# Merging a block-diagonal matrix into a weight: full float32r products by masked blocks, or float32 blocks of 32x32 side by side

## The chip, the cores and the metric

The kernel runs on one core of one Trainium2 chip. Its time is device microseconds for one execution; the time before is the median of three runs. TensorE is called PE (its weight loads PEld), VectorE DVE, ScalarE ACT, GpSimd POOL, and SyncE's queue SP.

## The reference

A layer norm of x, a linear attention with 32 heads of 32 channels, and a gated SwiGLU branch of the same normed x; their product is added to x:

```python
def reference(A_x, A_wqkv, A_wo, B_x, B_w1, B_w3, B_w2):
    def _A_ref(x, wqkv, wo):                      # x: 1 x 2048 x 1024
        H = 32; Dh = D // H
        q, k, v = ...                             # x @ wqkv, by heads
        phi = lambda t: jnp.where(t > 0, t + 1, jnp.exp(t)) + 1e-6
        pq, pk = phi(q), phi(k)
        kv = jnp.einsum("bhsd,bhse->bhde", pk, v)
        z = jnp.einsum("bhsd->bhd", pk)
        num = jnp.einsum("bhqd,bhde->bhqe", pq, kv)
        den = jnp.einsum("bhqd,bhd->bhq", pq, z)[..., None] + 1e-6
        o = num / den
        return o.transpose(0, 2, 1, 3).reshape(B, S, D) @ wo
    def _B_ref(x, w1, w3, w2):                    # w1, w3: 1024 x 3584
        ...
        return (silu(gate) * up) @ w2
    xn = _layernorm(x)
    s = _A_ref(xn, A_wqkv, A_wo)
    g = _silu(_B_ref(xn, B_w1, B_w3, B_w2))
    return x + s * g                              # x is A_x, before the norm
```

`kv` is one 32x32 matrix for each head. Because `o @ wo` is `(pq * 1/den) @ (blockdiag(kv) @ wo)`, the kernel first multiplies kv into wo (1024 x 1024), head by head, and calls that the merge.

## The kernel before, in words

Matmuls of the large products work on pairs of float32r numbers. `split` rounds a tile to a high part on ACT and takes the rest on DVE, and `mm3` issues three 128x128 by 128x512 matmuls: high by high, high by low, low by high (lines 109, 110, 111). The large products are done by a two-by-two scheme of seven products instead of eight; `PRODUCTS` = B11, T2, T3, T1, B21, T4, B22 names the right operands. They are B11, B21, B22 themselves and T1 = B12 - B11, T2 = B22 - T1, T3 = B22 - B12, T4 = B21 - T2.

The work goes through two halves of the rows of x. In the second half, queries and keys are followed by `row_products`, which makes the sums behind kv (kept in DRAM as `g_d`), and then by 14 pairs of `gemm`s for the gate and the up branch, each 7 x 12 = 84 full matmuls. A gemm takes banks of PSUM for its five accumulators, one (`ba`) at its start and four (`bb` to `be`) after its first product; operands of the next gemms are staged through further banks by `advance`. PSUM has eight banks in one pool (`ps`), shared by all.

Beside the gemms run jobs. They are generators; after each but the last of a gemm's seven products, `catch_up` lets the first job of the list go on to its next `yield`. One such step is called a turn here; a gemm has six. `attention_work` is the job that follows the row products. It divides the queries of the first row groups by their denominators (`divide`), makes and merges kv, and goes on with the other divisions; weight sums follow. `go_on` runs a list of `Job`s and asks for the loads of the next ones two or three ahead. Loads go to `job_tile`s, of which there are four, through SP's queue.

The merge before takes the eight column groups j one after another. `key_values(j)` multiplies g by the value weights as float32 matmuls of 128 x 32 weights, four of them side by side (line 1323, `tile_position=(0, g * DH)`), and DVE spreads the four 32x32 results under a mask `hmask` into a 128x128 block-diagonal `kvf`. `merge_wo` splits `kvf` and a 128-row strip of wo (`wos`), does one `mm3` for each half of the columns, and copies the result back to SBUF (`wo`, line 1356). When both strips of a k are there, POOL makes the four T's (`sums_of`, lines 1145 to 1149) and SP stores the seven products to `wp_d`, one DRAM tile for each four of them. When the second half is over, `attention_right` loads them (line 1623), and they are split into the right operands of the attention's last product.

The denominators (line 1258) are another group of small float32 matmuls: weights of 128 x 32, 256 columns, four side by side. The order of instructions on an engine is fixed when the kernel is built, by a planner that takes the code's order as priority.

Of the kernel before, what the change touches and what calls it, by code (L numbers as in the profile page):

```python
# [22 lines left out]
def tile_linear_attention_times_swiglu(  # L23
# [31 lines left out]
    make_identity(nc, ident)  # L55
    eps = const.tile([P, 1], F32, name="tiny")
    nc.vector.memset(eps, 1e-6)
    hmask = const.tile([P, P], F32, name="hmask")
    nc.vector.memset(hmask, 0.0)
    for i in range(P // DH):  # L60
        nc.vector.memset(hmask[i * DH:(i + 1) * DH, i * DH:(i + 1) * DH], 1.0)
# [19 lines left out]
    WROWS = [9, 6, 13, 24, 15, 11, 10, 21, 1, 16, 4, 18, 5, 8, 12, 20, 17, 25]  # L81
    WBLOCKS = {0: (1, 1), 2: (1, 0), 3: (2, 1), 7: (2, 0), 14: (0, 1), 22: (3, 0), 19: (2, 0), 23: (2, 1)}
    h_d = [dram.tile([P, len(HROWS), 2, NQ, P], F32, name=f"h_d{h}") for h in range(NH)]
    wp_d = [dram.tile([P, 4, C], F32, name=f"wp_d{g}") for g in range(7 * ND // 8)]
    wt_d = [dram.tile([P, len(WROWS), C], F32, name=f"wt_d{k}") for k in range(NQ)]
    qs_d = [dram.tile([P, 7, ND // 2, P], F32, name=f"qs_d{m}") for m in range(S // (2 * P))]
    r_d = [dram.tile([P, 2 * P], F32, name=f"r_d{m}") for m in range(S // (2 * P))]
# [517 lines left out]
                if next(job, None) is None:  # L605
                    jobs.pop(0)

    held = [0]

    def advance():  # L610
        if held[0]:
# [4 lines left out]
    def gemm(B, A, use, early=False, paired=False, own=False, led=False):  # L616

        name = B.name
        stays = name[0] == "u"

        B.upto("B11")
        u = (st.tile([P, C], F32, tag="own", bufs=1, name=f"u{name}") if own else
             pe.tile([P, C], F32, tag="u", name=f"u{name}"))
        ba = bank(f"a{name}")  # L630
        last = product(ba, B.upto("B11"), A["A11"], True)
        if early:
            yield
        copied = nc.scalar.copy(out=u, in_=ba)
        if early:
            yield
            product(ba, B.upto("B21"), A["A12"], False)
            yield
            yield from use.steps(0, 0, ba)
            yield  # L640
        else:
            advance()
            catch_up(copied, last)
            if paired:
                yield
        bb, bc, bd, be = (bank(f"{n}{name}") for n in "bcde")

        def settled(*marks):
            if not led:
                advance()  # L650
                catch_up(*marks)

        last = product(bb, B.upto("T2"), A["S2"], True)
        if led:
            yield
        added = nc.vector.tensor_add(out=u, in0=bb, in1=u)
        settled(copied, added, last)
        if paired or led:
            yield
        last = product(bc, B.upto("T3"), A["S3"], True)  # L660
        if led:
            yield
        c21 = small(f"c21{name}")
        c22 = bc if stays else small(f"c22{name}")
        added = nc.vector.tensor_add(out=c21, in0=bc, in1=u)
        settled(copied, added, last)
        if paired or led:
            yield
        last = product(bd, B.upto("T1"), A["S1"], True)
        if led:  # L670
            yield
        added = nc.vector.tensor_add(out=c22, in0=bd, in1=c21)
        if led:
            yield
        use(1, 1, c22)
        advance()
        catch_up(copied, added, last)
        if paired:
            yield
        if not early:  # L680
            last = product(ba, B.upto("B21"), A["A12"], False)
            use(0, 0, ba)
# [457 lines left out]
        store_rows(h, t, 16, r16)  # L1140
        yield

    def sums_of(b11, b12, b21, b22, e=nc.gpsimd):

        e.tensor_sub(out=b11, in0=b12, in1=b11)
        e.tensor_sub(out=b12, in0=b22, in1=b12)
        yield True
        e.tensor_sub(out=b22, in0=b22, in1=b11)
        e.tensor_sub(out=b21, in0=b21, in1=b22)

    def weight_sums(t, part, place=job_tile, e=pool, queue=nc.sync, slow=False):

        cols = slice(part * P, (part + 1) * P)
# [145 lines left out]

        return Job(load, steps)  # L1300

    kvf = {}

    def key_values(j):

        def load():
            g = job_tile([P, 2, ND // 2, P], f"g{j}")
            for e in range(2):
                nc.sync.dma_start(out=g[:, e], in_=g_d[2 * e + j % 2][:, :, j // 2 * P:(j // 2 + 1) * P])
            w = job_tile([P, 2, ND // 2, P], f"wv{j}")  # L1310
            rows = wqkv[:, 2 * D + j * P:2 * D + (j + 1) * P]
            nc.sync.dma_start(out=w.rearrange("p e k n -> p (e k) n"), in_=rows.rearrange("(k p) n -> p k n", p=P))
            return g, w

        def steps(both):
            yield True
            acc = bank(f"kv{j}")[:, :DH]
            g_, w_ = both
            for e in range(2):
                for k in range(ND // 2):  # L1320
                    for g in range(P // DH):
                        c = slice(g * DH, (g + 1) * DH)
                        nc.tensor.matmul(acc[c], lhsT=w_[:, e, k, c], rhs=g_[:, e, k, c], skip_group_check=True,
                                         start=e + k == 0, stop=bool(e) and k == ND // 2 - 1, tile_position=(0, g * DH))
# [6 lines left out]
        return [Job(load, steps)]  # L1331

    def merge_wo(k):

        both = []

        def load(e):
            j = k + e * (ND // 2)
            t = job_tile([P, 2, C], f"wo{j}")
            nc.sync.dma_start(out=t, in_=wo[j * P:(j + 1) * P, :].rearrange("p (n c) -> p n c", c=C))  # L1340
            return t

        def steps(e, t):
            both.append(t)
            j = k + e * (ND // 2)
            kvm = st.tile([P, 2, P], FR, tag="kvm", bufs=1, name=f"kvm{j}")
            split(kvm, kvf[j])
            o = []
            for n in range(2):
                o.append(operand([P, 2, C], FR, f"wos{j}_{n}"))  # L1350
                split(o[n], t[:, n])
                yield True
            for n in range(2):
                acc = bank(f"wp{j}_{n}")
                mm3(acc, (kvm[:, 0], kvm[:, 1]), (o[n][:, 0], o[n][:, 1]), True, True)
                nc.scalar.copy(out=t[:, n], in_=acc)
                yield True
            if e:
                b = [t[:, n] for t in both for n in range(2)]
                for n, i in (("B11", 0), ("B21", 2), ("B22", 3)):  # L1360
                    store(n, b[i])
                yield from sums_of(*b)
                for n, i in (("T1", 0), ("T3", 1), ("T4", 2), ("T2", 3)):
                    store(n, b[i])
                yield True

        def store(n, t):
            g, e = divmod(7 * k + PRODUCTS.index(n), 4)
            nc.sync.dma_start(out=wp_d[g][:, e], in_=t)

        return [Job(lambda e=e: load(e), lambda t, e=e: steps(e, t)) for e in range(2)]


    def all_denominators():
        yield from spread_z()
# [242 lines left out]
    def attention_right(n, i, k):  # L1618
        g, e = divmod(k * len(PRODUCTS) + i, 4)
        if g not in places:  # L1620
            raw = praw.tile([P, 4, C], F32, tag="raw", name=f"wpr{g}")
            for i in range(2):
                nc.sync.dma_start(out=raw[:, 2 * i:2 * i + 2], in_=wp_d[g][:, 2 * i:2 * i + 2])
            places[g] = raw, pa.tile([P, 4, 2, C], FR, tag=AOPS[g], name=f"wp{g}")
        return places[g][0][:, e]

# [186 lines left out]
```

## Time and profile before

| what | value |
|---|---|
| time, median of 3 runs (lowest to highest) | 2263.08 us (2261.74 to 2263.15) |
| the profiled execution | 2261.58 us, span 2259.8 us |
| busy: PE, PEld, DVE, ACT, POOL | 99%, 82%, 69%, 46%, 31% of the span |
| merge and key-values run | 1110 to 1300 us |
| merged weight stored, loaded | 1123.1 to 1300.3 us, 1581.0 to 1614.3 us |
| DMA | 495.18 MB, mean 219 GB/s |

Times in rows of the profile are microseconds from the span's start unless marked ns. A row of a group of instructions gives line, engine, operation, output and inputs, the count behind x, and the durations. A row of the timeline gives start, duration and what ran; in brackets stands the idle time before it and what ended that. SPq and ACTq rows are DMAs being issued, not their transfer. A matmul's duration includes the depth of its pipeline, so matmuls overlap in the record.

### The profile page before, as it was taken

What the parts mean: (1) busy time and instruction counts of PE and PEld (TensorE: products, weight loads), DVE (VectorE), ACT (ScalarE), POOL (GpSimd) and SP (SyncE); (2) the same over time, 40 slices, a digit from 0 to 9 for tenths busy, and PEclk for the clock granted to TensorE, in tenths of its full rate; (3) what the DMA queues carried; (4) which work ended last, traced back from release to release, by engine and by line L of the source; (5) the groups of instructions that cost most, each with busy time, mean ns of one, the idle gap of its engine ahead of it and who ended that gap; (6) DMA issues with size and microseconds to landing.
All of it is one profiled execution on the core that took longest, in us unless ns stands there. A gap on an engine that the chain in (4) does not pass through costs nothing.

```text
span 2259.8 us, 31282 instructions
## 1 busy us (share of the span) xinstructions
PE 2240.6 (99%) x10584; PEld 1844.9 (82%) x10584; DVE 1553.4 (69%) x2607; ACT 1044.8 (46%) x1780; POOL 696.5 (31%) x1163
## 2 busy tenths in 40 slices
PE   7999999999999999999999999999999999999998
PEld 6888888888888888778888888888888888888887
DVE  8987777665656776567766687856865555566576
ACT  6655454534343555434445443443522544444452
POOL 2220223377773621001244255478121000001010
PEclk9999999999999999999999999999999999999999
DMA  6555655677778745777766577877776856668595
GB/s 242 175 198 173 192 176 180 186 226 211 215 217 273 243 143 194 255 253 240 226 200 195 178 237 246 246 220 226 252 225 212 303 196 220 221 204 268 194 302 204
DMA packets 434657, 495.18 MB, mean 219 GB/s; under 512 B 22192, under 2 KB 328112, under 8 KB 434384
## 3 DMA queue, kind: packets, MB, share of 16 engines
q1 hardware_dynamic: 352112, 353.44, 49.4%
q0 software_dynamic: 26080, 82.99, 11.2%
q10 hardware_dynamic: 56304, 56.76, 8.0%
q8 instruction: 83, 1.36, 0.2%
q14 instruction: 78, 0.64, 0.1%
HBM read 315.62 MB, written 181.14 MB: 220 GB/s over the span
## 4 chain that ended last, share of the span: by engine, by line
PE 98%; DVE 1%; DMA 1%; issue 0%; ACT 0%; DVEq 0%
PE o L111 7%; PE o L110 7%; PE o L109 7%; PE g L109 2%; PE g L110 2%; PE g L111 2%; PE trk L716 1%; PE as L109 1%; PE ds L109 1%; PE cs L109 1%; PE ds L111 1%; PE cs L111 1%; PE as L110 1%; PE ds L110 1%; PE cs L110 1%; PE as L111 1%
## 5 line engine op out<-in xcount | busy, mean ns | idle before, releaser
L109 PE MATMUL o<-w,l 128*128 128x512 f32 x728 | 283.2, 389 | 0.0
L110 PE MATMUL o<-w,l 128*128 128x512 f32 x728 | 283.2, 389 | 0.0
L111 PE MATMUL o<-w,l 128*128 128x512 f32 x728 | 283.2, 389 | 0.0
L103 ACT CAST l<-lr 128x896 fp32r<-128x896 f32 (+1 forms) x106 | 98.5, 932 | 203.8 <-PE o L111 104.0
L104 DVE TENSOR_TENSOR l<-lr,l 128x896 fp32r<-128x896 f32 (+1 forms) x106 | 113.6, 1073 | 81.6 <-ACT l L103 80.3
L110 PEld LDWEIGHTS o<-w,l 128*128 128x128 f32 x728 | 136.6, 188 | 28.4
L109 PEld LDWEIGHTS o<-w,l 128*128 128x128 f32 x728 | 136.6, 188 | 28.4
L111 PEld LDWEIGHTS o<-w,l 128*128 128x128 f32 x728 | 136.6, 188 | 28.3
L1577 POOL DMA_DIRECT2D out<-acc x14 | 12.0, 860 | 397.6 <-DVE acc L1575 397.6
L104 DVE TENSOR_TENSOR xy<-xy,xy 128x512 fp32r<-128x512 f32 x112 | 73.1, 687 | 59.0 <-ACT xy L103 59.0
L103 ACT CAST xy<-xy 128x512 fp32r<-128x512 f32 x112 | 64.9, 620 | 96.2 <-PE g L111 74.2
L1787 DVE TENSOR_TENSOR acc<-o,acc 128x512 f32<-128x512 f32 x63 | 43.1, 690 | 87.9 <-PE o L111 87.9
L993 POOL TENSOR_TENSOR hs<-h,h 128x128 f32<-128x128 f32 x104 | 48.0, 482 | 142.1 <-DVE h L977 142.1
L110 PE MATMUL g<-xy,xy 128*128 128x512 f32 x224 | 87.5, 391 | 0.0
L111 PE MATMUL g<-xy,xy 128*128 128x512 f32 x224 | 87.2, 389 | 0.0
L109 PE MATMUL g<-xy,xy 128*128 128x512 f32 x224 | 80.5, 394 | 0.3 <-DVE gc L855 0.3
L993 POOL TENSOR_TENSOR hs<-h,hs 128x128 f32<-128x128 f32 (+1 forms) x130 | 73.6, 586 | 22.9 <-DMA h_d<-hs 20.0
L993 POOL TENSOR_TENSOR w2s<-w 128x256 f32<-128x256 f32 x75 | 54.4, 739 | 55.6 <-DMA wt_d<-w2s 54.5
L720 POOL DMA_DIRECT2D y_d<-y x48 | 34.6, 723 | 117.8 <-ACT y L747 43.0
L104 DVE TENSOR_TENSOR w<-wr,w 128x512 fp32r<-128x512 f32 x98 | 63.1, 686 | 11.1 <-ACT w L103 11.1
L103 ACT CAST w<-wr 128x512 fp32r<-128x512 f32 x98 | 57.8, 620 | 20.7 <-DMA wr<-in_B_w 15.2
L102 DVE SCALAR_TENSOR_TENSOR w<-wr,w 128x512 fp32r<-128x512 f32 x84 | 53.8, 687 | 4.1 <-ACT w L101 4.0
(5645 smaller groups left out, 6868.9 us busy)
## 6 DMA issues: line engine op xcount, KB each, us to landing
lr<-h_d SPq DMA_DIRECT2D x102, 448.0 KB
wr<-wt_d SPq DMA_DIRECT2D x126, 256.0 KB
wt_d<-w2s SPq DMA_DIRECT2D x50, 512.0 KB
h_d<-hs SPq DMA_DIRECT2D x96, 256.0 KB
w<-in_B_w SPq DMA_DIRECT2D x56, 256.0 KB
xy<-x_d SPq DMA_DIRECT2D x28, 512.0 KB
xy<-y_d SPq DMA_DIRECT2D x28, 512.0 KB
wr<-in_B_w SPq DMA_DIRECT2D x56, 256.0 KB
```

The source lines that it names most:

```text
L102: return nc.vector.scalar_tensor_tensor(lo, src, -1.0, hi.bitcast(F32), op0=ALU.mult, op1=ALU.subtract)
L103: nc.scalar.copy(out=hi, in_=src)
L104: return nc.vector.tensor_sub(out=lo, in0=src, in1=hi.bitcast(F32))
L109: nc.tensor.matmul(acc, lhsT=wh, rhs=ah, start=start, stop=False, skip_group_check=True)
L110: nc.tensor.matmul(acc, lhsT=wh, rhs=al, start=False, stop=False, skip_group_check=True)
L111: return nc.tensor.matmul(acc, lhsT=wl, rhs=ah, start=False, stop=stop, skip_group_check=True)
L716: nc.tensor.transpose(p_[:, t * P:(t + 1) * P], src[:, t * P:(t + 1) * P], ident)
L720: nc.gpsimd.dma_start(out=y_d[h][:, :, YS.index(n), pair], in_=t.rearrange("p (t d) -> p t d", d=P))
L993: self.last = getattr(self.e, name)(**how)
L1577: nc.gpsimd.dma_start(out=out[rows, cols], in_=a, accum_op=ALU.add)
L1787: nc.vector.tensor_add(out=a, in0=b, in1=a)
```

## The change

`key_values` now copies its four 32x32 results as they are, 128 x 32, to one tile `kv` for all j. The mask is gone. `merge_wo` comes after all eight, in two parts of 256 columns of each half of wo. A part loads its share of wo as four tiles of 128 x 4 x 256 (for two halves e of the rows and two halves n of the columns). `blocks(e, both)` multiplies each head's 32x32 kv by the 32 rows of wo that belong to it, as float32 matmuls without splitting. A head lies at rows r of the array; its result goes to the partitions of j, so that each of the 16 places (r, j) has a matmul of its own, and the r-th bank of four collects the heads at r. ACT copies the banks back into the wo tiles, now with (j, d) as partition and r beside it. The part waits with `blocks` for a gemm's first turn (`begins`).

T1 and T4 are made by POOL as before; T2 and T3 are subtracted on DVE from the PSUM banks of the second half. Stores go to one DRAM tile `wp_d` of [4, 128, 7, 512], and the loads for the last product put the rows into the old order; where two neighbouring products belong to different k, the load is in two.

```diff
-    hmask = const.tile([P, P], F32, name="hmask")
-    nc.vector.memset(hmask, 0.0)
-    for i in range(P // DH):
-        nc.vector.memset(hmask[i * DH:(i + 1) * DH, i * DH:(i + 1) * DH], 1.0)
...
-    wp_d = [dram.tile([P, 4, C], F32, name=f"wp_d{g}") for g in range(7 * ND // 8)]
+    wp_d = dram.tile([P // DH, P, 7, C], F32, name="wp_d")
...
             advance()
+            begins[0] = True
             catch_up(copied, last)
+            begins[0] = False
...
-            kvf[j] = st.tile([P, P], F32, tag="kvf", bufs=1, name=f"kvf{j}")
-            heads = [P, P // DH, DH]
-            nc.vector.tensor_mul(kvf[j].rearrange("p (g c) -> p g c", c=DH),
-                                 acc.unsqueeze(1).to_broadcast(heads), hmask.rearrange("p (g c) -> p g c", c=DH))
-            yield True
+            nc.vector.tensor_copy(out=kv_[:, j], in_=acc)
+            yield True
...
+    def merge_wo(kv_, part):
+        cols = slice(part * 2 * P, (part + 1) * 2 * P)
+        R = range(P // DH)
         def load(e):
+            rows = wo[e * C:(e + 1) * C, :].rearrange("(j p) (n c) -> n p j c", p=P, c=C)
+            both = [job_tile([P, P // DH, 2 * P], f"wo{part}_{e}{n}") for n in range(2)]
+            for n, t in enumerate(both):
+                nc.sync.dma_start(out=t, in_=rows[n][:, :, cols])
+            return both
         def store(n, t):
+            dst = wp_d[:, :, PRODUCTS.index(n), cols]
+            nc.sync.dma_start(out=dst.rearrange("r p c -> p r c"), in_=t)
+        def blocks(e, both):
+            accs = [bank(f"wp{part}{e}_{r}").rearrange("p (n c) -> p n c", n=2) for r in R]
+            for n, t in enumerate(both):
+                for j in R:
+                    for r in R:
+                        here = slice(r * DH, (r + 1) * DH)
+                        nc.tensor.matmul(accs[r][j * DH:(j + 1) * DH, n], lhsT=kv_[here, e * (ND // 2) + j], rhs=t[here, j],
+                                         start=True, stop=True, skip_group_check=True, tile_position=(r * DH, j * DH))
+            for r in R:
+                for n, t in enumerate(both):
+                    nc.scalar.copy(out=t[:, r], in_=accs[r][:, n])
+            return accs
+        (b11, b12), (b21, b22) = both = load(0), load(1)
+        for _ in range(3):
+            yield True
+        while not begins[0]:
+            yield True
+        blocks(0, both[0])
+        yield True
+        store("B11", b11)
+        yield True
+        yield True
+        pool.tensor_sub(out=b11, in0=b12, in1=b11)
+        yield True
+        store("T1", b11)
+        yield True
+        while not begins[0]:
+            yield True
+        accs = blocks(1, both[1])
+        for r in R:
+            nc.vector.tensor_sub(out=b12[:, r], in0=accs[r][:, 1], in1=b12[:, r])
+            nc.vector.tensor_sub(out=b11[:, r], in0=accs[r][:, 1], in1=b11[:, r])
+        yield True
+        for n, t in (("B21", b21), ("B22", b22), ("T3", b12), ("T2", b11)):
+            store(n, t)
+        yield True
+        yield True
+        pool.tensor_sub(out=b21, in0=b21, in1=b11)
+        yield True
+        store("T4", b21)
...
-        work = []
-        for k in range(ND // 2):
-            for e, j in enumerate(merge_wo(k)):
-                work += key_values(k + e * (ND // 2)) + [j]
-        yield from go_on(work)
+        kv = st.tile([P, ND, DH], F32, tag="kv", bufs=1, name="kv")
+        yield from go_on([key_values(j, kv) for j in range(ND)])
+        for part in range(2):
+            yield from merge_wo(kv, part)
...
-            for i in range(2):
-                nc.sync.dma_start(out=raw[:, 2 * i:2 * i + 2], in_=wp_d[g][:, 2 * i:2 * i + 2])
+            for q in range(0, 4, 2):
+                (k0, i0), (k1, i1) = (divmod(4 * g + q + x, len(PRODUCTS)) for x in range(2))
+                for x, k_, i_, n_ in ((q, k0, i0, 2),) if k0 == k1 else ((q, k0, i0, 1), (q + 1, k1, i1, 1)):
+                    rows = wp_d[:, k_ * DH:(k_ + 1) * DH, i_:i_ + n_]
+                    nc.sync.dma_start(out=raw[:, x:x + n_], in_=bass.AP(
+                        tensor=rows.tensor, offset=rows.offset,
+                        ap=[[P * len(PRODUCTS) * C, P // DH], [len(PRODUCTS) * C, DH], [1, n_ * C]]))
```

More of the change, by code (lines that the diff above doesn't have):

```diff
@@ L606, in catch_up @@
                     jobs.pop(0)
-    held = [0]
+    held, begins = [0], [False]
     def advance():
@@ L1141, in sums_steps @@
         yield
-    def sums_of(b11, b12, b21, b22, e=nc.gpsimd):
-        e.tensor_sub(out=b11, in0=b12, in1=b11)
-        e.tensor_sub(out=b12, in0=b22, in1=b12)
-        yield True
-        e.tensor_sub(out=b22, in0=b22, in1=b11)
-        e.tensor_sub(out=b21, in0=b21, in1=b22)
     def weight_sums(t, part, place=job_tile, e=pool, queue=nc.sync, slow=False):
@@ L1300, in divide, with key_values @@
         return Job(load, steps)
-    kvf = {}
-    def key_values(j):
+    def key_values(j, kv_):
         def load():
@@ L1324, in steps @@
                                          start=e + k == 0, stop=bool(e) and k == ND // 2 - 1, tile_position=(0, g * DH))
-            kvf[j] = st.tile([P, P], F32, tag="kvf", bufs=1, name=f"kvf{j}")
-            heads = [P, P // DH, DH]
-            nc.vector.tensor_mul(kvf[j].rearrange("p (g c) -> p g c", c=DH),
-                                 acc.unsqueeze(1).to_broadcast(heads), hmask.rearrange("p (g c) -> p g c", c=DH))
+            nc.vector.tensor_copy(out=kv_[:, j], in_=acc)
             yield True
-        return [Job(load, steps)]
@@ L1333, in merge_wo @@
-    def merge_wo(k):
-        both = []
+        return Job(load, steps)
+    def merge_wo(kv_, part):
+        cols = slice(part * 2 * P, (part + 1) * 2 * P)
+        R = range(P // DH)
         def load(e):
[L1338 to L1365, printed above, removed]
-        def store(n, t):
-            g, e = divmod(7 * k + PRODUCTS.index(n), 4)
-            nc.sync.dma_start(out=wp_d[g][:, e], in_=t)
-        return [Job(lambda e=e: load(e), lambda t, e=e: steps(e, t)) for e in range(2)]
@@ L1374, in all_denominators @@
+        yield True
[7 more added lines that the diff above has]
+        yield True
+        yield True
     def all_denominators():
```

## The prediction

> **What bounds the kernel now.** I read the page first (busy shares, granted clock, chain), then the matrix engine's waits, then the stretch in which the merge runs.
>
> ```profile
> span 2259.8 us, 31282 instructions
> PE 2240.6 (99%) x10584; PEld 1844.9 (82%) x10584; DVE 1553.4 (69%) x2607; ACT 1044.8 (46%) x1780; POOL 696.5 (31%) x1163
> PEclk9999999999999999999999999999999999999999
> PE 98%; DVE 1%; DMA 1%; issue 0%; ACT 0%; DVEq 0%
> ```
> ```profile
> PE tA L296 <- ACT xa L285: 11.1, 2, 10.6
> PE ak__323 L110 <- DVE A L308: 0.8, 1, 0.8
> PE tS L296 <- DVE S L308: 0.5, 1, 0.5
> PE ak__379 L109 <- ACT uk__378 L634: 0.4, 1, 0.4
> PE g L109 <- DVE gc L855: 0.3, 1, 0.3
> ```
> ```profile
> 1092.30:1301.60 209.30, 209.30 (x1402) 171.33 (x1402) 136.75 (x227) 98.36 (x180) 75.80 (x113) 1.00 0.64 199
> 1054.30:1092.30 38.00, 38.00 (x169) 31.50 (x168) 32.80 (x68) 18.72 (x32) 8.95 (x15) 1.00 0.69 213
> ```
>
> The chain that ended last is 98% PE, the clock is full throughout, and after the first tens of microseconds PE waits for next to nothing (the list above is complete but for shorter entries). So what the change is worth is what it takes out of or puts into PE's own stream, unless it makes PE wait where it never did. The two stretches (columns: time, then busy time of PE, PEld, DVE, ACT, POOL, clock, DMA share) are two gemms with no job in between, 19.0 us each (84 matmuls, so 0.226 us a matmul), and the ten gemms beside which the key-values and the merge run. There PE is full too, and ten gemms take 209.3 - 190.0 = 19.3 us more than bare ones: those 19.3 us are the jobs. DVE (65%), ACT (47%), POOL (36%) and the DMA engines (0.64) have room.
>
> **The change, part by part.**
>
> ```profile
> L109 PE MATMUL wp<-wos,kvm x16: 392/392/393, 1120.9 to 1293.1; 128*128 128x512 f32 x16
> 1120.90 0.39 PE L109 MATMUL wp<-wos,kvm 128*128 128x512 f32 x1
> 1121.13 0.40 PE L109 MATMUL du__10290<-S,T1u__10169 128*128 128x512 f32 x1
> ...
> 1130.06 0.39 PE L111 MATMUL eu__10291<-A,T4u__10307 128*128 128x512 f32 x1
> 1130.38 0.76 PE L1323 MATMUL kv<-g,wv 128*32 128x32 f32 x64
> 1131.07 0.51 PE L109 MATMUL du__10290<-S,B22u__10329 128*128 128x512 f32 x1
> 1131.41 0.39 PE L110 MATMUL du__10290<-S,B22u__10329 128*128 128x512 f32 x1
> ```
>
> *Removed from PE.* The merge is 3 x 16 full matmuls (lines 109 to 111). A matmul's duration (0.39) holds its pipeline; what it occupies is the distance to the next start, 1121.13 - 1120.90 = 0.23. So 48 x 0.23 = 11.0 us go. Cross-check: a key-value group pushes the stream back by 1131.41 - 1130.06 less two normal steps, 1.35 - 0.45 = 0.90 us, eight of them 7.2; 19.3 - 7.2 = 12.1 is the most the merge can be. I take 11.0. The key-value groups stay as they are.
>
> *Added to PE.* Four blocks (two parts, two halves e), each of 2 x 4 x 4 = 32 float32 matmuls with 32x32 weights and 256 columns, on all 16 places (r, j). No matmul of before uses a row group alone. The nearest rows are the denominators: float32, 256 columns, four column groups side by side.
>
> ```profile
> L1258 PE MATMUL den<-pqd,zb x128: 379/379/403, 907.8 to 1032.2; 128*32 128x256 f32 x128
> 907.29 0.39 PE L110 MATMUL g<-xy,xy 128*128 128x512 f32 x1
> 907.52 0.39 PE L111 MATMUL g<-xy,xy 128*128 128x512 f32 x1
> 907.83 0.59 PEld L1258 LDWEIGHTS den<-pqd,zb 128*32 128x32 f32 x16 [0.35 <-issue]
> 907.83 1.07 PE L1258 MATMUL den<-pqd,zb 128*32 128x256 f32 x16
> 908.84 0.50 PE L109 MATMUL g<-xy,xy 128*128 128x512 f32 x1
> 909.18 0.40 PE L110 MATMUL g<-xy,xy 128*128 128x512 f32 x1
> ```
>
> The code issues 64 denominator matmuls and the trace has 128 records: two records for a float32 matmul, 0.379 us each. Sixteen such records end within 1.07 us, so four run at once: four rounds, of (1.07 - 0.38) / 3 = 0.23 us. The whole group with the way in and out pushes the stream back by 909.18 - 907.52 = 1.66 less 0.45, 1.21 us; the way in and out is 1.21 - 4 x 0.23 = 0.29 of it. A block has 64 records; if all 16 places run at once, that is four rounds again, and 1.21 us. The feeding isn't the limit: the key-value group passed 64 records in 0.90 us. So the ends are 0.90 a block (feeding alone), and 1.21 + 12 x 0.23 = 3.97 if only four run at once. I take 1.21, since the rows show that different places of the array overlap and only the number of places differs: 4 x 1.21 = 4.8 us.
>
> The Trainium skill, "TensorE: Matmul & The Clock Gate" (Part 3: Packing small matmuls, the measured speedups), gives 10.6 times for 16 places at once; as an estimate from that page, a block would be 64 x 0.23 / 10.6 + 0.29 = 1.7 us and the sum below -4.3 us instead of -6.2. No run here shows it yet.
>
> *Sum on PE:* -11.0 + 4.8 = -6.2 us.
>
> *DVE, ACT, POOL.* Gone are 16 splits of wo, 8 of the key-values, 16 copies and 8 masks; the last rows give their prices.
>
> ```profile
> L103 ACT CAST wos<-wo x16: 620/622/625, 1116.1 to 1287.0; 128x512 fp32r<-128x512 f32 x16
> L104 DVE TENSOR_TENSOR wos<-wo,wos x16: 681/692/807, 1116.8 to 1287.6; 128x512 fp32r<-128x512 f32 x16
> L1356 ACT COPY wo<-wp x16: 586/588/605, 1122.5 to 1294.3; 128x512 f32<-128x512 f32 x16
> L1145 POOL TENSOR_TENSOR wo<-wo x4: 1292/1294/1302, 1127.8 to 1275.5; 128x512 f32<-128x512 f32 x4
> L1589 DVE TENSOR_TENSOR acc<-o,acc 128x256 f32<-128x256 f32 x2 | 0.8, 420 | 1.9 <-PE o L111 1.9
> ```
>
> ACT loses 16 x 0.62 + 16 x 0.59 = 19.4 us and more, and gains 32 copies of 128x256, at most 32 x 0.42 = 13.4. DVE loses 16 x 0.69 = 11.1, gains 16 subtractions from PSUM of the form that took 0.42, 6.7. POOL goes from 16 subtractions of 1.29 to 4 of twice the size, 20.7 to about 10.4. Worth nothing, as none of the three is the bound; the cover is their idle share above. What matters is the burst: at a block, ACT has 8 copies in a row (some 3 us), and after the second half DVE another 8 x 0.42 = 3.4 us reading the same four banks. A block takes four of the eight PSUM banks at once, where the merge took one, and keeps them 3 to 6 us. It is called only at a gemm's first job turn, when the gemm holds one bank and staged operands, and the next two products (12 x 0.226 = 2.7 us each) need one new bank each. So I cost the banks at nothing; that cover is thin, and it is a rival below.
>
> *DMA and queues.*
>
> ```profile
> L1369 SPq DMA_DIRECT2D wp_d<-wo x28: 319/323/545, 1123.1 to 1300.3; - x28
> L1623 SPq DMA_DIRECT2D wpr<-wp_d x14: 319/400/1085, 1581.0 to 1614.3; - x14
> 1123.11 0.34 SPq L1369 DMA_DIRECT2D wp_d<-wo  x1
> 1127.80 1.29 POOL L1145 TENSOR_TENSOR wo<-wo 128x512 f32<-128x512 f32 x1 [17.38 <-DMA wp_d<-wo]
> 1182.57 0.74 POOL L993 TENSOR_TENSOR h<-h,hs_a 128x256 f32<-128x256 f32 x1
> 1197.58 1.30 POOL L1146 TENSOR_TENSOR wo<-wo,wo 128x512 f32<-128x512 f32 x1 [14.28 <-ACT wo L1356]
> ```
>
> The bytes stay. Stores become 14 of 512 KB in 1 KB pieces instead of 28 of 256 KB in 2 KB pieces; loads of wo stay 8 of 512 KB, in 1 KB pieces; SP issues 14 stores fewer. The reordered loads are 16 instead of 14, since the pairs (6, 7) and (20, 21) cross a row block: 2 x 0.40 us on SP's queue, 280 us after the last store. A dearer piece would raise a DMA share of 0.64, with a third to spare; cost nothing. The job's turns: the merge part shrinks from 56 turns (16 for key-values, 40) to about 50 by the code, so divisions and weight sums behind it start no later.
>
> *The mask at the start.*
>
> ```profile
> 1.09 0.47 DVE L61 MEMSET hmask<- 32x32 f32 x4
> 4.27 1.28 DVE L147 BATCH_NORM_STATS2 bs<-xa 128x6 f32<-128x512 f32 x2 [2.33 <-DMA xa<-in_A_x]
> ```
>
> The memsets are over before DVE sits 2.33 us for the first rows: worth nothing. All tiles behind the mask move by 512 bytes; I see no price for that.
>
> **The rivals.**
>
> *Main case, 55%:* -6.2 us. The profiled execution took 2261.58 us (span 2259.8), 1.5 under the median of 2263.08. So 2255.4 against the profiled one, 2256.9 against the median. Own range 2255.5 to 2258.5 (0.90 a block gives 2255.7; a block cut in two by a matmul of the gemm pays the 0.29 of way in and out twice, in all four 2258.1).
>
> *PE waits at the blocks, or the blocks fall apart, 22%:* banks come one by one, or wo, now four 512 KB loads asked for at once and some four turns ahead, lands late; PE's order is fixed, so it stands. Before, a merge matmul alternated with the gemm's, as the rows at 1120.90 and 1121.13 show, which costs a full-width matmul nothing; a 32x32 one pays the change of mode. At 0.5 to 2 us a block: 2258.9 to 2264.9. For it: four banks instead of one. Against: not one wait of PE from the merge before.
>
> *Four at once, 9%:* matmuls that share a row or a column group take turns. 16 rounds: 4 x 3.97 = 15.9, +4.9 us, 2268.0. For it: before shows only column groups. The row above has 16 loads of weights in 0.59 us, inside the 1.07 us of matmuls that use the same 128 rows, so sharing rows doesn't hold a load back here. The same page of the Trainium skill (Part 3, the mechanism) says that a weight load overlaps running matmuls only where the row groups differ; by that rule j = 1 would wait for j = 0, which is this case. The trace of the column groups speaks against it: its loads overlap, on the same rows.
>
> *One at a time, 3%:* 64 rounds, 1.21 + 60 x 0.23 = 15.0 a block, 60 in all, +49: 2312.
>
> *The second block waits for T1's store, 6%, slower:* DVE may overwrite b11 with T2 only when T1, made by POOL, has left. The store of B11 took 1127.80 - 1123.11 = 4.7 us to let POOL go on, for half the bytes; POOL is free for 14 us in such a place (rows at 1182.57 and 1197.58). B11 stored, T1 made (2.6) and stored, at up to 9 us a store, is 24 us after the first block with its copies; the second comes one gemm, 21 us, later and is copied 4 us after that. If the stores take 4 us more each, DVE stands with four banks held; from about 8 us of standing (three products) PE stands too, and twice 6 us more turn -6.2 into +6: 2269.
>
> *More gained, 5%:* the neighbours of the merge also speed up (12.1 instead of 11.0) and blocks cost 0.90: -8.5, 2254.6.
>
> **How the numbers follow.** 0.2% is 4.5 us here, about what a measurement can tell. Faster: nearly all of the main case, the 5%, a little of the waits: 58%. Within 0.2%: most of the waits, half of four at once, a little of the main case: 28%. Slower: the other half, one at a time, T1's store: 14%. Time 2256.9. The range 2254.5 to 2265 holds the main case, the gain beyond it and the waits, 82%, and leaves out the cases beyond.
>
> **What will show it.** Right: four groups of 64 records of form 32x32 on PE, each about 1.1 us long, stepping the stream by 1.2 us; the ten gemms' stretch takes about 203 us; PE's list of waits stays as short as it is. Wrong: records of a block in rounds of four (a group of 3.8 us); a block broken up between gemm matmuls; new entries of PE waiting for ACT, DVE or wo near the blocks; DVE waiting there for the store of T1.

## The result, and the profile after

The kernel got slower: 2299.68 us median of five runs (2299.18 to 2302.01) against 2262.84 us for five runs of the kernel before (2261.74 to 2263.15). The ratio is 1.0165, 95% interval 1.015 to 1.018. The forecast was 2256.9 us and its range ended at 2265.

First the page after: span, busy time, granted clock in 40 slices, and the chain that ended last.

```profile
span 2298.0 us, 31642 instructions
PE 2251.9 (98%) x10792; PEld 1845.8 (80%) x10792; DVE 1546.0 (67%) x2594; ACT 1034.9 (45%) x1772; POOL 684.9 (30%) x1151
PEclk9999999999999999999999999999699999999999
PE 86%; DMA 8%; POOL 3%; DVE 2%; issue 1%; ACT 0%; SPq 0%; DVEq 0%; POOLq 0%; ACTq 0%
```

Before, the chain was 98% PE and the clock row was all nines. Now 8% of the chain is DMA (by the page's next row 2% are the loads of the merged weight, `wpr<-wp_d`; the rest are other transfers along the chain), and one slice of the clock stands at 6. It is the 29th of 40, 1609 to 1666 us: not the place of the merge (1110 to 1300 us), but the place where the merged weight is loaded and split. PE's list of waits says the same, by its longest entries after the start-up ones:

```profile
PE T3s L104 <- ACT XS3s L98: 7.9, 1, 7.9
PE T2s L104 <- ACT wp L98: 3.7, 1, 3.7
PE B21s L104 <- ACT XA12s L98: 3.4, 1, 3.4
PE B21s L104 <- ACT wp L98: 2.9, 1, 2.9
PE T1s L104 <- ACT wp L98: 2.7, 1, 2.7
PE T4s L104 <- ACT wp L98: 2.7, 1, 2.7
```

Each is a product of the attention's last matmuls, and ACT, which PE waits for, waits for the loads itself: `XS3s` and `XA12s` are casts that stand on ACT right behind a split of `wp`. The loads (issue rows, and what the splitting engines sat idle for), and then the splits of `wp`, after:

```profile
L1628 SPq DMA_DIRECT2D wpr<-wp_d x16: 507/508/3857, 1571.5 to 1639.0; - x16
DMA wpr<-wp_d: 49.7, 14
1621.15 1.14 ACT L98 CAST wp<-wpr 128x512 fp32r<-128x512 f32 x2 [3.39 <-DMA wpr<-wp_d]
1626.35 1.14 ACT L98 CAST wp<-wpr 128x512 fp32r<-128x512 f32 x2 [3.55 <-DMA wpr<-wp_d]
1631.40 1.14 ACT L98 CAST wp<-wpr 128x512 fp32r<-128x512 f32 x2 [3.39 <-DMA wpr<-wp_d]
```

ACT splits two products whenever a load of 512 KB lands, and that is every 5.1 us (1631.40 - 1626.35 = 5.05 and 1626.35 - 1621.15 = 5.20). The queue of these loads is the only one with much to do in 1600 to 1640 us. Its packets, MB and share of the 16 engines there, after:

```profile
q1 hardware_dynamic: 1242, 4.08, 25.6%
```

and in 1600 to 1616 us before, where the last of the loads run:

```profile
q1 hardware_dynamic: 988, 3.62, 65.5%
```

25.6% of 16 engines is 4.1: the loads ran steadily on four engines. In the trace's records of single pieces four of these are under way at a time (a fifth only for the few ns in which one piece follows another), 0.16 us for a piece of 4 KB; 128 pieces on four engines are 32 x 0.16 = 5.1 us, the distance between ACT's casts. Before, up to 16 are under way, with holes between loads. The trace's records of completions say it a second way: each load of before reports 16, each of the changed kernel one at its issue and four when data land. The load's new pattern is `[4, 32, 1024]` where the old one began with 128 rows.

The stretches from 1560 and from 1630 us, before (first fence) and after (columns: time, then PE, PEld, DVE, ACT, POOL, clock, DMA share, GB/s):

```profile
1560.00:1630.00 70.00, 70.00 (x310) 57.95 (x310) 56.35 (x100) 38.69 (x70) 27.68 (x44) 1.00 0.76 244
1630.00:1760.00 130.00, 130.00 (x576) 107.63 (x575) 79.69 (x158) 34.71 (x60) 28.21 (x45) 1.00 0.66 214
```
```profile
1560.00:1630.00 70.00, 58.71 (x239) 47.09 (x238) 41.20 (x66) 27.25 (x49) 13.01 (x20) 0.90 0.38 134
1630.00:1760.00 130.00, 116.55 (x472) 91.83 (x472) 78.13 (x166) 36.42 (x62) 28.14 (x43) 0.91 0.68 219
```

PE stood for 70 - 58.71 = 11.3 and 130 - 116.55 = 13.4 us, 24.7 in all. The account by the first matmul of each gemm in the two traces: after the merge the new kernel is 4.2 us ahead, at the start of the last gemm still 0.95 us, at the end 38.36 us behind. So 39.3 us were lost in these stretches: 24.7 as standing, and the other 14.6 as matmuls that started further apart. The timeline of PE after shows the second kind:

```profile
1624.93 0.63 PE L104 MATMUL T3s<-wp,XS3s 128*128 128x512 f32 x1
1625.36 0.63 PE L105 MATMUL T3s<-wp,XS3s 128*128 128x512 f32 x1
...
1629.14 0.39 PE L106 MATMUL B21s<-wp,XA12s 128*128 128x512 f32 x1
1629.37 0.39 PE L105 MATMUL B11s<-wp,XA11s 128*128 128x512 f32 x1
```

Here PE's wait had ended at 1622.86; from 1624.1 to 1627.5 us the steps are 0.43 us, and then 0.23 again.

The merge itself, after, a block in the timeline and the ten gemms' stretch between the same two gemm starts as in the prediction:

```profile
1179.21 0.39 PE L106 MATMUL ag__11001<-A,B11g__10940 128*128 128x512 f32 x1
1179.53 1.49 PE L1339 MATMUL wp<-wo,kv 32*32 32x256 f32 x64
1180.96 0.50 PE L104 MATMUL bg__11064<-S,T2g__10977 128*128 128x512 f32 x1
1181.29 0.40 PE L105 MATMUL bg__11064<-S,T2g__10977 128*128 128x512 f32 x1
```
```profile
1093.10:1297.40 204.30, 204.30 (x1610) 165.26 (x1609) 130.80 (x230) 88.06 (x172) 66.14 (x106) 1.00 0.70 213
```

The four blocks are unbroken groups of 64 records, PE is full, and the stretch fell from 209.3 to 204.3 us: the merge brought 5.0 us. A block pushes the stream back by 1181.29 - 1179.21 = 2.08 less two steps of 0.225, 1.63 us.

### The profile page after: what moved, and what is told of

It reads as the page before. It is cut to its first block, busy times and chain, and to the rows that moved or that the text cites. A ratio compares the mean times of both kernels' runs of the same rounds, so it can differ in the third digit from the quotient of the medians.

```text
span 2298.0 us, 31642 instructions
## 1 busy us (share of the span) xinstructions
PE 2251.9 (98%) x10792; PEld 1845.8 (80%) x10792; DVE 1546.0 (67%) x2594; ACT 1034.9 (45%) x1772; POOL 684.9 (30%) x1151
## 3 DMA queue, kind: packets, MB, share of 16 engines
q0 software_dynamic: 26080, 82.99, 10.9%
## 4 chain that ended last, share of the span: by engine, by line
PE 86%; DMA 8%; POOL 3%; DVE 2%; issue 1%; ACT 0%; SPq 0%; DVEq 0%; POOLq 0%; ACTq 0%
PE o L105 7%; PE o L106 7%; PE o L104 7%; DMA wpr<-wp_d 2%; PE g L104 2%; PE g L105 2%; PE g L106 2%; DMA h_d<-hs 2%; POOL hs L990 1%; POOL w2s L990 1%; DMA wt_d<-w2s 1%; DMA h_d<-h 1%; PE trk L713 1%; PE as L106 1%; PE cs L104 1%
```

## The experiments

Theory: the loads' leading 4 confines them to four engines, and the merge itself is a gain. Rivals: the stores in 1 KB pieces or the merge's banks do the harm; or the gain of the merge isn't real.

**Each ordered load cut in four.** The changed kernel, with a load for each r, so that each has 32 contiguous-row pieces and no leading 4:

```diff
-                    rows = wp_d[:, k_ * DH:(k_ + 1) * DH, i_:i_ + n_]
-                    nc.sync.dma_start(out=raw[:, x:x + n_], in_=bass.AP(...))
+                    for r in range(P // DH):
+                        nc.sync.dma_start(out=raw[r * DH:(r + 1) * DH, x:x + n_],
+                                          in_=wp_d[r, k_ * DH:(k_ + 1) * DH, i_:i_ + n_])
```

> The changed kernel with each ordered load cut into four, one for each row block r (32 partitions from 32 rows). Same bytes, same addresses, same places. Theory E (engines): the load of the changed kernel moved with 4 pieces in flight because its access pattern begins with a dimension of 4, and 16 such loads of 5.1 us each starved PE; cut by r every load begins with 32, so up to 16 pieces are in flight, the loads take about 35 us together again as before the change, PE's waits for wp go, and the time is about 2262.8 - 4.5 (merge) + 2.8 (two new waits of PE at 1409 and 1552) = 2258 to 2262 us. Rival A (addresses: rows 14 KB apart in four places of one DRAM tile are slow to read, or the stores' tile as a whole holds the loads up): the time stays at 2290 to 2300. Rival M (the merge and its banks cost): stays above 2280 with fast loads.

Measured: 2266.83 us against 2263.41, ratio 1.0017 [1.0008, 1.0026]. 33 of the 37 us are back, with the same bytes at the same addresses and the same stores, so neither the distance between the rows nor the 1 KB pieces of the stores had cost them. PE's waits that are left, and the queue (the loads as a group, then the rows of the queries, and the same issue in the kernel before):

```profile
PE du__13190 L104 <- DVE cu__13189 L669: 3.2, 1, 3.2
PE as L106 <- DVE XA11s L99: 2.3, 1, 2.3
```
```profile
L1628 SPq DMA_DIRECT2D wpr<-wp_d x64: 302/419/1539, 1574.7 to 1622.2; - x64
1623.46 0.82 SPq L1535 DMA_DIRECT2D r0q<-qs_d  x2
```
```profile
1616.98 0.80 SPq L1533 DMA_DIRECT2D r0q<-qs_d  x2
```

No wait of PE for `wp` is left. But SP has 64 of these issues instead of 16, 0.42 us each (27 us in all; the rest of the 48 us up to 1622.7 are waits of the queue, 15.4 us of it in one place), and the rows of the queries (`r0q`) are asked for behind them, 6.5 us later than before. The wait at `as` is for these rows' split; with the slow steps behind it, it takes 4.2 us. The other, at 1410 us, takes 5.1 us with its slow steps, 165 us ahead of these loads. So the cut undoes the loss, but isn't free, and the time lies 4.8 us above what was expected.

**The leading 4 alone, in the kernel before.** First by writing its 128 contiguous rows as 4 x 32, 8 x 16 and 2 x 64, nothing else changed:

```diff
-                nc.sync.dma_start(out=raw[:, 2 * i:2 * i + 2], in_=wp_d[g][:, 2 * i:2 * i + 2])
+                rows = wp_d[g][:, 2 * i:2 * i + 2]
+                nc.sync.dma_start(out=raw[:, 2 * i:2 * i + 2], in_=bass.AP(
+                    tensor=rows.tensor, offset=rows.offset,
+                    ap=[[P // 4 * 4 * C, 4], [4 * C, P // 4], [1, 2 * C]]))
```

> The kernel before with only the pattern of its loads of the merged weight changed: the same contiguous rows, written as 4 blocks of 32 instead of 128. Theory E: 4 pieces in flight, 5.1 us a load, 14 loads 72 us instead of about 35: 30 to 40 us slower than before, with PE's clock down in that stretch. Rival A: no change (2262.8), since addresses and order are those of before. If the pattern is merged to 128 rows on the way, 16 in flight and no change, which the trace would show in the pieces in flight.

> As the run before it, written as 8 blocks of 16. Theory E: 8 pieces in flight, 2.6 us a load, 14 loads 36 us, about as long as they take now with all waits: 0 to 8 us slower than before. Rival A: no change.

> As 2 blocks of 64. Theory E: 2 pieces in flight, 10.2 us a load, 14 loads 143 us: some 105 us slower than before, 2360 to 2380 us. Rival A: no change.

Measured: 2263.21 us for 4 x 32, ratio 0.9999 [0.999, 1.0009]; one run each of 8 x 16 and 2 x 64, 2262.79 and 2261.75 us. The queue of 4 x 32 in 1600 to 1616 us:

```profile
q1 hardware_dynamic: 1035, 3.78, 67.9%
```

This is the share of before (65.5%), with up to 16 pieces under way. The distance between the groups was the distance between rows times their count, so the two dimensions can be written as one. They already were in the instruction: its record in the trace has the shape of before (`dst_num_elem=[128,1]`), where those of the changed kernel have `[1,128]`. So no pattern that begins with 4, 8 or 2 was run, and these three say nothing on the theory. The pattern of the change can't be joined: each group of `wp_d` has 128 rows, and a load takes 32 of them.

So the DRAM tile was given a row of padding behind each 32, which keeps the two dimensions apart; the old merge stays, its stores are cut in four to leave the padding out.

```diff
-    wp_d = [dram.tile([P, 4, C], F32, name=f"wp_d{g}") for g in range(7 * ND // 8)]
+    wp_d = [dram.tile([4, DH + 1, 4, C], F32, name=f"wp_d{g}") for g in range(7 * ND // 8)]
...
-            nc.sync.dma_start(out=wp_d[g][:, e], in_=t)
+            for r in range(4):
+                nc.sync.dma_start(out=wp_d[g][r, :DH, e], in_=t[r * DH:(r + 1) * DH])
...
+                    ap=[[(DH + 1) * 4 * C, 4], [4 * C, DH], [1, 2 * C]]))
```

> The kernel before with its old merge; the merged weight is kept in DRAM in 4 blocks of 32 rows with an unused row behind each, so that the loads' pattern of 4 x 32 can't become 128 rows. Stores are cut by block, 32 partitions each, loads are 14 as before. Theory E: 4 pieces in flight in the loads, about 5.1 us a load, 72 us for 14, PE waits for wp and the clock goes down there: 2290 to 2302. Rival A (the addresses far apart, the new tile, the merge): no change, 2263.

Measured: 2306.43 us against 2262.72, ratio 1.0194 [1.0179, 1.021]. PE's waits and the loads' queue in 1600 to 1640 us:

```profile
PE T3s L109 <- ACT XS3s L103: 8.0, 1, 8.0
PE B21s L109 <- ACT XA12s L103: 3.6, 1, 3.6
```
```profile
q1 hardware_dynamic: 1041, 4.14, 25.5%
```

The two waits stood at 7.9 and 3.4 us in the changed kernel, and the queue's share at 25.6%: the kernel before, with its old merge, is 43.7 us late at the end, by a pattern that begins with 4. 5.0 of them it had lost at the start of the last gemm, mostly in two waits, which ended at 1339.6 and 1418.3 us; the other 38.6 are lost in the loads' stretch, as 39.3 were in the changed kernel. This shows the cause without the new merge. The time was 4 us above what was expected.

**Two engines instead of four.** The changed kernel, each load cut into two of `[2, 32, ...]`:

```diff
+                    for h in range(2):
+                        rows = wp_d[2 * h:2 * h + 2, k_ * DH:(k_ + 1) * DH, i_:i_ + n_]
...
+                            ap=[[P * len(PRODUCTS) * C, 2], [len(PRODUCTS) * C, DH], [1, n_ * C]]))
```

> The changed kernel with each ordered load cut into two, each of 2 blocks of 32 rows. Theory E: 2 pieces in flight, so a load takes twice as long as in the changed kernel, 10.2 us, and 16 of them 164 us: 70 to 85 us more than the changed kernel, 2370 to 2385. Rival A: 2300 or a little less, since the transfers are cut smaller and nothing else changes.

Measured, in one run: 2363.71 us. The queue in 1600 to 1640 us, and ACT's splits:

```profile
q1 hardware_dynamic: 649, 2.05, 12.9%
```
```profile
1640.16 1.14 ACT L98 CAST wp<-wpr 128x512 fp32r<-128x512 f32 x2 [8.97 <-DMA wpr<-wp_d]
1650.41 1.14 ACT L98 CAST wp<-wpr 128x512 fp32r<-128x512 f32 x2 [8.59 <-DMA wpr<-wp_d]
```

12.9% is 2.1 engines, and 512 KB take 10.2 us, twice 5.1. Two loads side by side did not get four engines: never more than two pieces are under way for longer than a few ns, and the loads of 256 KB issued at 1593.8, 1596.1 and 1601.0 us landed one after another, at 1611.9, 1614.6 and 1617.2. So they went through the same two. The dose is clear: 16, 4 and 2 engines give 2263, 2300 and 2364 us. The loss was 6 us under the lower end of what was expected.

The Trainium skill, "DMA: Bandwidth & Descriptors" (section "Why a DMA increments its semaphore by 16 and not by 1"), states this rule: a transfer uses the largest number of engines up to 16 that divides the slowest dimension above one of both patterns. These traces agree: 4.1 engines for a leading 4, 2.1 for a leading 2.

**Order in the stores.** The new merge, with `wp_d` as before and the old 14 loads; the row order is made by the stores, each cut in four by the column group j:

```diff
-            dst = wp_d[:, :, PRODUCTS.index(n), cols]
-            nc.sync.dma_start(out=dst.rearrange("r p c -> p r c"), in_=t)
+            for j in R:
+                g, e = divmod(7 * j + PRODUCTS.index(n), 4)
+                nc.sync.dma_start(out=wp_d[g][:, e, cols].rearrange("(r d) c -> d r c", d=DH),
+                                  in_=t[j * DH:(j + 1) * DH])
```

> The changed kernel's merge, but the row order is made when storing: each store cut into four by j (32 partitions, 4 x 256 each), so that the merged weight lies as before the change and is loaded by the 14 plain loads of 128 rows. Theory E: 16 pieces in flight in the loads, no waits of PE for wp, and SP has 14 loads to issue there, not 64, so the next rows come as early as before. The merge's own gain, 5.0 us by the gemms' starts in the changed kernel (0.8 us late at the first gemm beside the jobs, 4.2 us early after the merge), shows at the end less what PE waits for at about 1410 us (0 to 5 us, seen in kernels with either merge): 2257.5 to 2262.5. Rival M (the merge costs more than its gain): not below 2263.

Measured: 2262.49 us against 2262.72, ratio 0.9996 [0.9987, 1.0005]. The loss is gone, but so is the gain (the profiled execution took 2260.93; the eleven lie between 2258.85 and 2264.38). By the starts of the gemms the merge brings its 5.0 us here too (1.2 us behind before it, 3.8 ahead after it); then 1.9 us go at 1410 us and 1.1 at 1552. PE's waits there, then what DVE waits for at the first, then the longest step of the chain in 1395 to 1415 us (start, duration, what):

```profile
PE du__13238 L104 <- DVE cu__13237 L669: 1.7, 1, 1.7
PE cu__14712 L104 <- ACT T3u__14677 L467: 0.6, 1, 0.6
```
```profile
DVE c21u__13282 L662 <- DMA h_d<-hs: 3.2, 1, 3.2
```
```profile
1397.24 10.90 DMA h_d<-hs
```

A store of 256 KB of the hidden rows (`h_d<-hs`) takes 10.9 us to let its tile go, and DVE needs the tile for the next product. The wait isn't new:

```profile
DVE c21u__13209 L665 <- DMA h_d<-hs: 3.5, 1, 3.5
```

is a row of the kernel before. It has no part in the prediction, as PE didn't stall behind it. Beside these stores runs `divide`, whose load of the denominators (`qd<-r_d`) has the pattern `[4, 32 repeats, 512]`: a leading 4 again, in the kernel before too.

**The order of a block's matmuls.** The last kernel with r outside j, so that successive matmuls share a row group instead of a column group:

```diff
-                for j in R:
-                    for r in R:
+                for r in R:
+                    for j in R:
```

> As the cut stores, with the blocks' matmuls in the order n, r, j instead of n, j, r: neighbours in the stream share the row group r and differ in the column group. If weight loads wait for matmuls of the same row group, a block takes longer than the 1.49 us and the 1.63 us of step that it takes in the changed kernel; about 3.9 us if four run at once. If only the places count, both stay within 0.1 us.

Measured, in one run: 2260.82 us, and a block is the same to the last digit: 1.49 us long, a step of 1.63 us. The order, and so which groups neighbours share, makes no difference here.

**The division's load cut in four.** Added to the kernel with the order in the stores, and, as a control, to the kernel before alone:

```diff
-                nc.sync.dma_start(out=t[:, 2:], in_=bass.AP(
-                    tensor=rows.tensor, offset=rows.offset, ap=[[4 * P, P // DH], [0, DH], [1, 4 * P]]))
+                for g in range(P // DH):
+                    nc.sync.dma_start(out=t[g * DH:(g + 1) * DH, 2:], in_=bass.AP(
+                        tensor=rows.tensor, offset=rows.offset + g * 4 * P, ap=[[0, DH], [1, 4 * P]]))
```

> The kernel after, with the row order made in the stores (each cut in four by the column group j) and the loads as before, and in addition the division's repeated rows (qd<-r_d, one load whose pattern begins with 4, so four pieces at once) cut into four loads, one for each group of 32 rows. Theory A (the 5 us that the merge saves are given back at 1410 us because the four engines that carry qd<-r_d hold up the stores h_d<-hs, for which VectorE waits 3.2 us there): the stall before du at 1410 goes, and with it 1.9 us; 2258 to 2261, the step of the gemm starts stays near -3.8 us until 1550. Theory B (the stall there is a matter of order, any small shift moves it, and the qd loads don't matter): the stall stays or another takes its place, 2261 to 2264; the 48 DMA instructions more on SP's queue may add a stall of their own.

> The kernel before with only the division's repeated rows cut into four loads. Theory A: PE didn't stall at 1410 us before, so nothing to gain: 2262 to 2264, and VectorE's wait for h_d<-hs (3.5 us) gets shorter. Theory B: the same time and the same wait of VectorE.

Measured: 2258.00 us with the new merge, ratio 0.9977 [0.9969, 0.9986]; 2262.01 us for the control, ratio 0.9994 [0.9985, 1.0003]; both against 2263.27. DVE's longest wait in 1305 to 1440 us, with the new merge and then in the control:

```profile
DVE B22u__12961 L468 <- ACT B22u__12961 L467: 2.5, 1, 2.5
```
```profile
DVE B22u__12879 L473 <- ACT B22u__12879 L472: 2.5, 1, 2.5
```

The wait for `h_d<-hs` has left both lists. Between 1000 and 1700 us PE has one wait left with the new merge:

```profile
PE g L104 <- DVE gc L852: 0.6, 1, 0.6
```

and from the merge on it is 3.7 to 3.8 us ahead, to the end. The trace's records of completions show what the cut changed. A store of `hs` reports 16. With the order in the stores, twelve of them come 2.4 to 5.3 us after the issue (all 20 stores of 1305 to 1440 us), and the last only after 4.3 to 11.1 us; for the store issued at 1397.24, twelve were in by 1400.7 and the last four came from 1407.4 to 1408.1. In the kernel before it is twelve and four as well. With the load cut, in both kernels, the 13th comes within 0.2 us of the 12th; with the new merge the last comes after 2.8 to 7.4 us. So four of the sixteen shares of each store stood behind the division's load: the same leading 4, in a load that the change doesn't touch, held up the stores beside it and took back part of the merge's gain. Alone, the cut brings nothing that can be told from zero, as PE wasn't waiting there. Why the wait at 1552 went with it was not tried by itself.

**A block of half as many matmuls.** In the trace's single records the first 32 of a block start within 0.34 us. The 33rd starts at 0.46, the 34th at 0.65, and from there most come 16.7 ns apart, until 1.12, close behind a load of weights: the second half n uses the places again, with the same weights loaded once more. So, on top of the kernel with the division's load cut, both halves n were put into one matmul of 512 columns (the tiles of wo hold two j and both n each, so each is loaded in two parts):

```diff
-            for n, t in enumerate(both):
-                for j in R:
-                    for r in R:
-                        ...matmul(accs[r][j * DH:(j + 1) * DH, n], ..., rhs=t[here, j], ...)
+            for j in R:
+                t = both[j // 2].rearrange("p (n x) c -> p n x c", n=2)
+                for r in R:
+                        ...matmul(accs[r][j * DH:(j + 1) * DH], ..., rhs=t[here, :, j % 2], ...)
```

> The kernel e12_cut_divide, and each place's two matmuls of 256 columns (one for each half n of wo's columns, with the same weights loaded twice) made one of 512 columns, so 16 matmuls a block instead of 32. Theory A (a block costs 1.63 us and not the 1.21 us of the prediction because the second half's weights can't go onto a place until the matmul there has run out, a hole of 0.19 us and loads 16.7 ns apart after it): 32 records a block, no hole, a step of 1.15 to 1.3 us, so 1.3 to 1.9 us less in all; 2256 to 2257. Theory B (a block is bound by the columns that go through, and the hole is only where its way out shows): the step stays at 1.55 to 1.7 us and the time at 2258. ScalarE's first copies come at most 0.3 us later, since each tile is now read to the block's end.

Measured: 2255.94 us against 2262.89, ratio 0.9969 [0.9957, 0.9981], the fastest of all. The timeline of a block:

```profile
1179.47 0.39 PE L106 MATMUL ag__11035<-A,B11g__10974 128*128 128x512 f32 x1
1179.79 1.22 PE L1343 MATMUL wp<-wo,kv 32*32 32x512 f32 x32
1180.94 0.50 PE L104 MATMUL bg__11082<-S,T2g__11011 128*128 128x512 f32 x1
1181.27 0.39 PE L105 MATMUL bg__11082<-S,T2g__11011 128*128 128x512 f32 x1
```

A step of 1181.27 - 1179.47 - 0.45 = 1.35 us instead of 1.63, for the same products; 1.35 is just over the 1.15 to 1.3 that was expected. Four steps give 1.1 of the 2.1 us by which this kernel is below the one with the load cut. What in the second half costs the 0.28 us is not shown: the edit takes away the second loads of weights and half of all the records at once. Reloading alone isn't dear everywhere, for the four rounds of the denominators in the prediction have new weights for every matmul too, and in the single records they start 0.22 to 0.24 us apart, without a hole.

## Why the prediction was wrong

**The step that failed** stands under "DMA and queues": "The reordered loads are 16 instead of 14 ...: 2 x 0.40 us on SP's queue" and "A dearer piece would raise a DMA share of 0.64, with a third to spare; cost nothing". The loads were priced by their number, bytes and piece size, and the 512 KB by the time of before. What had changed was the first dimension of the pattern, from 128 to 4. The share of all engines could not show it: four full engines out of 16 look like a quarter of the load. With 5.1 us for 512 KB the 14 x 512 KB take 71 us. That is the step that was wrong: at a quarter of the engines the loads' transfer, put at nothing, held PE back from 1604 to 1664 us. How much time they had stands in these rows of before:

```profile
L109 PE MATMUL B11s<-wp,XA11s x4: 389/389/389, 1603.8 to 1620.8; 128*128 128x512 f32 x4
L103 ACT CAST wp<-wpr x28: 611/618/622, 1591.4 to 1620.0; 128x512 fp32r<-128x512 f32 x28
```

PE used the first of them 23 us after the first issue (1581.0) and all were split by 1621. The cover that I named (280 us after the last store) lies ahead of the loads; behind them there is hardly any. The spans differ by 2298.0 - 2259.8 = 38.2 us: 39.3 lost here, 5.0 gained by the merge, the rest (3.9) mostly stalls at 1410 and 1552 us (3.2) and what was lost ahead of the merge (0.8). No rival had this place: all that could end slower sat at the merge. The signs that I listed as wrong were all near the blocks as well.

**Removed from PE, added to PE:** right in kind. Four groups of 64 records, unbroken, all 16 places at once, 204.3 us for the ten gemms where about 203 was forecast, so -5.0 and not -6.2. The term that was off is the block: 1.63 us, not 1.21, in all 1.7 us. I took rounds of 0.23 from the denominators' row, and the second half of a block doesn't follow that row; with one matmul of 512 columns at each place a block took 1.35, and the stretch 203.3. The estimate from the Trainium skill, 1.7 us a block ("TensorE: Matmul & The Clock Gate", Part 3), was nearer than the one from the denominators' row, and the trace agrees with it (1.63 us); as the same products took 1.35 us with 512 columns a matmul, part of that is luck. The 48 removed matmuls at 0.23 come out as 5.0 + 4 x 1.63 = 11.5 us if the key-values cost what they did, between the 11.0 taken and the 12.1 that was the most.

**The rival "four at once"** (a load overlaps only across row groups) is refuted: a block is 1.49 us long and not near 4, and the order of rows and columns changes nothing. **PE waits at the blocks:** none; the four banks cost nothing. **The second block waits for T1's store:** the mechanism's first half was there, on POOL after:

```profile
POOL wo L990 <- DMA wp_d<-wo: 34.2, 3, 18.0
```

POOL stood up to 18.0 us for a store (17.4 before); but DVE has no wait for a store of `wp_d` at the second blocks, and PE none.

**DVE, ACT, POOL, the mask:** as forecast, nothing; all three are a little less busy than before.

**The end at which it came out** was outside the range since the range was made of prices at the merge alone. With the order made elsewhere the forecast of 2256.9 stands against 2262.5 measured, and against 2258.0 with the division's loads cut as well: the thin slack of the stores at 1410 us was the second thing not seen. Its row, DVE's wait of 3.5 us for `h_d<-hs`, was there before.

## What to carry to other kernels

When a change rewrites a DMA's pattern, price the first dimension of it, not only bytes, pieces and issues: a load that begins with 4 ran at a quarter of the engines and took 5.1 us for 512 KB, and cutting it, or moving the reordering to stores that begin with 32, gave back nearly all that this had cost. Look for such patterns in the kernel as it stands too, and for waits of an engine that end just before PE needs it: they cost nothing yet, but can take back the gain of what makes PE faster. A moved DMA is to be priced at the place where its data are needed, however far that is from the edit.

## What was not expected of the hardware

- Two dimensions that can be joined to one were joined before they reached the queue: 4 x 32 contiguous rows ran like 128 (67.9% of the engines); with one row of padding between the groups, 25.5%.
- Loads with a leading 2, several at a time, shared the same two engines (12.9%). What runs beside such loads is held up too, by just the engines that they use: beside the division's loads twelve of a store's sixteen shares were in after 3.4 us and the last four after 10.1 to 10.9, and DVE's wait for it vanished when these loads were cut.
- After a stall PE's steps are nearly twice as long for a while (the clock row falls with them). With each ordered load cut in four, eight matmuls started 0.43 us apart, 1.7 us more, behind a stall of 3.4 us at 1410 us and again behind one of 2.5 us at 1632, where the granted clock reads 0.50 from 1632.6 to 1636.0. Behind one of 2.5 us at 1418 (the padded tile) there was none, so the length alone doesn't decide. A wait of PE so can cost more than its row says: 14.6 of the 39.3 us here.
- 32 float32 matmuls of 32x32 weights and 256 columns on 16 places took 1.63 us of the stream whatever their order; 16 of 512 columns took 1.35.
